# SBUF tiles on multiples of 128 bytes, small loads merged into one, and a fifth buffer for h, in a kernel of a spectral layer and two MLPs

## The chip, the core and the metric

The kernel runs on one NeuronCore of one Trainium2 chip. The metric is device time in microseconds (us) of one execution; lower is better. Times of several executions are given as a median with the lowest and the highest.

## The reference, cut to what matters

```python
def _attn_ref(x) -> np.ndarray:
    X = np.fft.fft(x, axis=1)
    X = np.fft.fft(X, axis=2)
    return X.real.astype(np.float32)
...
def _moe_ref(x, w_in, w_out) -> np.ndarray:
    h = x @ w_in
    r = np.maximum(h, 0.0)
    g = r * r
    return (g @ w_out).astype(np.float32)
...
def _moe2_ref(x, w_in, w_out) -> np.ndarray:
    h = x @ w_in
    g = h * (1.0 / (1.0 + np.exp(-1.702 * h)))
    return (g @ w_out).astype(np.float32)
```

The input x is 2 x 3008 x 256 in float32. The real part of its Fourier transform over positions and features gives 6016 tokens of 256 features. These go through an MLP with relu squared (weights 256 x 2048 and 2048 x 256) and then through one with a sigmoid gelu (the same sizes). Weights arrive as 64-bit floats and are narrowed on the chip.

## The kernel before, in words

Everything lies in SBUF as [128 partitions, columns]. Each partition holds a row of bytes, and pools take pieces of that row from the left end or from the right end.

The kernel has three stages, and they overlap. First, for each of the two batches, the positions are folded by VectorE (ops f0 to f5, lines 486 to 540), transformed by TensorE in plain float32 (lines 559, 571 and 643) and split into a high and a low float32r part, tile `eo` (pool `ep`). Then comes the first MLP: 96 units F0 to F95. A unit takes 128 hidden features of one block of tokens. A block is 2 x 512 tokens (64 units) or 2 x 482 tokens (32 units). A unit has 6 front matmuls (lines 770 to 772, moving operand `eo`) and 12 back matmuls (line 785, moving operands `gh` and `gl`, pool `mg`), each 512 or 482 columns wide in float32r. Between front and back, VectorE adds (op P, lines 1049 to 1052, into `h`), ScalarE or VectorE does relu and square (op R, lines 1058, or 1060 and 1061), ScalarE rounds to the high part (op H, line 1066), and GpSimd or VectorE makes the low part (op G, line 179). The back matmuls come three units later, so three units are left over at the end (`drain`). The second MLP has 48 units of 21 matmuls in line 1105 (moving operands `ya`, `yb`, `yc`) and 24 in line 1121 (moving operands `gh`, `gl` of pools `m2` and `m3`); 32 of these units are 512 columns wide and 16 are 482.

The order of all work up to the second MLP is written out by hand in `ORDER`: each engine's queue follows it, with the name of a unit or an op per item. `HOME` says which engine does an op where it isn't the usual one (V VectorE, A ScalarE, G GpSimd), and `RINGS` says which buffer of a group a tile takes. All DMAs are issued from SyncE's queue (SP) in the same order. The second MLP's order stands in its loop (lines 1131 to 1206).

Where tiles lie follows from the sizes. From the left: 1,024 bytes of DMA scratch, four constants of 32 bytes each, 1,344 bytes of pool `small`, then pools `winp` and `wq` (weights in float32r), all in pieces of 8,192 bytes; the first of these begins at byte 2,496, which is 64 above a multiple of 128. The right side ends at byte 229,344, which is 96 above a multiple of 128. Pools `mg`, `m`, `ep` and `np` are stacked downwards from there in pieces of 2,048, 4,096 or 8,192 bytes, so each of their tiles begins 96 above a multiple of 128. In the second MLP a 32-byte tile `edge` (line 1206) puts `m3` at 64 above a multiple of 128; `m2`, on the left, is at 64 too. The 376-column matmuls of line 747 read `eo` from column 106 on, that is 96 + 424 = 520 bytes, 8 above a multiple of 128.

Of the kernel before, what the change touches and what calls it, by code (L numbers as in the profile page):

```python
# [9 lines left out]
F32 = mybir.dt.float32  # L10
# [9 lines left out]
CW = 380  # L20
# [19 lines left out]
f0e0 f2a0 nA nL i0A f2m f2p nC seD f1E f1O f1e1 f2u i0L f0e1 c00D i0C i0O f2E f1e0 u0D nO f0o i0S f2e0 c01D i0P f1o e00N  # L40
i1D e00n ma f2O i0M f2o e00m f1g e00E u0L c02D u0A nS c03D i0N e00c u0O e01E u0C i0H u0S e01N e01c e00s f2e1 e01s e00h
u1D e00l i0l e01h e01n e01l i1L u0P nP f2g i1O u0H o0E0
F0 e01hb
F1 o0c0 c10D i1A u0l e01m u1A P0 P1 o0s0
F2 f0g R0 o0E1
F3 se e01lb H0 P2 i2D R1 o0c1 o0s1 o02hb o02h i1C G0 o02l P3 B0 o02lb H1 G1
F4 i1S R2 H2 o02N o02n G2 R3 u1C P4 H3 i1P R4 B1 f3D G3 H4
F5
F6 P5 B2 c12D u1L i1N B3 G4 P6 i1M u1O
F7 u1S R5 X3.0 X3.1 i1H u2D B4 R6 H5 i1l u1P P7 G5 H6 R7  # L50
F8
F9 P8 G6 R8 B5 P9 i2L
F10 H7 R9 i2A H8 P10 B6 G7 i2C
F11 u1H P11 H9
F12 R10
F13 u1l i2S i2O G8 G9 i2P P12 H10 P13 B7 B8 u2A R11 H11 u2L i2N B9
F14 i2M G10 B10 G11 R12 u2C i2H R13 i3D i2l H12
F15 P14 H13 i3A u2O B11 G12 G13
F16 X11.0 P15 R14 i3C u2S i3L
F17 X11.1 H14 G14 R15 B12 i3S u2P P16 u2H u3D B13  # L60
F18 u2l R16 i3O H15 B14 P17 P18
F19 H16 i3P
F20 G15 R17 P19 R18 H17 B15 H18 G16 i3M
# [60 lines left out]
F81 B74 P80 R78 B75 H77 v1S
F82 G77 v1L P81 H78 G78 v1O jlD R79 B76 H79 R80 R81 P82
F83 B77 G79 H80 H81 v1P R82
F84 G80 v1H B78 B79 G81 P83 P84 H82
F85 R83 X79.1
F86 G82 P85 X79.0 v1l R84 P86 B80 y0 H83 H84 G83 R85 B81 R86
F87  # L130
F88 B82 y1 P87 H85 G84
F89 R87 P88 G85
F90 P89 R88 B83 B84 H86 G86 ybH0
F91 B85 H87 H88 G87 P90 R89 P91 y2 ybl0
F92 G88 B86 H89
F93 G89 R90 P92 ybH1 P93 H90 yaH R91 B87
F94 B88 G90 ybl1 R92 H91 R93 G91
F95 yal y3 H92 P94 B89 P95 B90 H93 R94 R95 H94 G92 G93 B91 B92 H95 G94 G95
"""
RINGS = {  # L140
    "a0": "0101010101101010101010101010101010101010101011010101010101010101010101010101010100101010101010100010"
          "1010101010101010",
    "a1": "0110010101010101010101010101010101010101011010101101010101010101010101010101010101010101010101010101"
# [3 lines left out]
    "h": "0123021302130302130213023210321032031203120312031203120312031203120313120312031203120313120312031203"  # L147
          "1203311203120312",
    "p": "0111110101010101010101010101010101010101010101010101010101010101010101010101010101010101010101010101"
# [1196 lines left out]
```

## Time and profile before

| | |
|---|---|
| median of 3 runs | 954.26 us (954.04 to 956.01) |
| the profiled execution | 956.24 us |
| span of its trace | 954.4 us |
| TensorE matmul busy | 943.6 us, 99% of the span |
| TensorE weight load busy | 776.5 us, 81% |
| VectorE busy | 685.8 us, 72% |
| ScalarE busy | 572.8 us, 60% |
| GpSimd busy | 273.8 us, 29% |
| granted TensorE clock, mean over the span | 1.00 of full speed (2.4 GHz) |

The span is the time between the first and the last instruction of the program; 1.84 us of the profiled execution lie around it. PE is TensorE, PEld its weight load, DVE VectorE, ACT ScalarE, POOL GpSimd, SP SyncE's queue of DMAs. Matmuls are pipelined: the duration shown for one is longer than the distance between two starts, so the pace is read from starts, or from pieces of the chain that hold many matmuls.

### The profile page before, as it was taken

The page shows a single profiled execution, that of the slowest core. Times are in us where ns is not written, and L with a number is a line of the kernel's source. Part 1 is how long each engine was busy: PE and PEld are TensorE (multiplying, and loading weights), DVE is VectorE, ACT ScalarE, POOL GpSimd, SP SyncE. Part 2 cuts the span into 40 slices and gives each one's busy share as a digit, 9 for nine tenths or more (in the row PEclk, how much of TensorE's full clock was granted, in tenths as well). Part 3 has the DMA queues.
Part 4 walks back from the last instruction along what each step waited for, and adds up shares of the span by engine and source line. Part 5 has one row for each costly group of instructions (what it writes and reads, how often), then busy time and mean ns, then how long its engine had stood idle before and what let it go on. Part 6 is the DMA issues. An engine that isn't in the chain of part 4 may idle for free.

```text
span 954.4 us, 10920 instructions
## 1 busy us (share of the span) xinstructions
PE 943.6 (99%) x4272; PEld 776.5 (81%) x4272; DVE 685.8 (72%) x796; ACT 572.8 (60%) x613; POOL 273.8 (29%) x150
## 2 busy tenths in 40 slices
PE   8999999999999999999999999999999999999998
PEld 8668888887878878888788888888888888888886
DVE  7899998977767886758797755655565575566453
ACT  3779988566765868676765644644554455455343
POOL 0445665443266646474104200030020002000000
PEclk9999999999999999999999999999999999999999
DMA  7721222520110030110320110020010011000001
GB/s 285 270 89 45 88 89 89 202 88 25 45 42 1 1 133 1 45 45 1 109 110 1 42 45 1 3 86 1 0 65 22 1 42 45 0 1 37 8 1 41
DMA packets 13347, 53.47 MB, mean 56 GB/s; under 512 B 1520, under 2 KB 4976, under 8 KB 10096
## 3 DMA queue, kind: packets, MB, share of 16 engines
q1 hardware_dynamic: 13296, 52.78, 15.3%
q8 instruction: 33, 0.54, 0.2%
q14 instruction: 18, 0.15, 0.1%
HBM read 37.29 MB, written 15.48 MB: 55 GB/s over the span
## 4 chain that ended last, share of the span: by engine, by line
PE 93%; DVE 4%; DMA 1%; ACT 1%; issue 0%; POOL 0%; SPq 0%; DVEq 0%
PE psb L1121 27%; PE psb L785 26%; PE psc L1105 23%; PE psa L770 4%; PE psa L772 4%; PE psa L771 4%; PE psa L643 2%; PE psa L571 1%; DMA xt<-in_x 1%; PE psb L643 1%; DVE h L1052 0%; DVE h L1051 0%; DVE p L1049 0%; PE psb L571 0%; DVE h L1058 0%
## 5 line engine op out<-in xcount | busy, mean ns | idle before, releaser
L785 PE MATMUL psb<-gh,w 128*128 128x512 f32 (+1 forms) x768 | 219.0, 391 | 0.4 <-ACT o L275 0.4
L179 POOL TENSOR_TENSOR gl<-h,gh 128x1024 fp32r<-128x1024 f32 (+1 forms) x68 | 169.9, 2500 | 162.4 <-PE psb L785 72.8
L785 PEld LDWEIGHTS psb<-gh,w 128*128 128x128 f32 x768 | 143.4, 188 | 32.6 <-ACT o L275 1.2
L1121 PE MATMUL psb<-gh,w 128*128 128x512 f32 (+1 forms) x576 | 164.3, 387 | 0.0
L1185 DVE TENSOR_TENSOR g<-u,psc 128x1024 f32<-128x1024 f32 (+1 forms) x48 | 57.6, 1200 | 117.0 <-PE psc L1105 117.0
L1187 ACT ACTIVATE g<-g 128x1536 f32<-128x1536 f32 (+1 forms) x48 | 70.4, 1467 | 94.6 <-DVE g L1185 94.6
L1066 ACT CAST gh<-h 128x1024 fp32r<-128x1024 f32 (+1 forms) x96 | 97.9, 1030 | 47.3 <-PE psb L785 33.9
L1121 PEld LDWEIGHTS psb<-gh,w 128*128 128x128 f32 x576 | 108.3, 188 | 21.0
L785 PE MATMUL psb<-gl,w 128*128 128x512 f32 (+1 forms) x384 | 119.0, 391 | 0.0
L179 DVE TENSOR_TENSOR gl<-g,gh 128x2048 fp32r<-128x2048 f32 (+1 forms) x48 | 110.5, 2302 | 1.3 <-ACT gh L1162 1.3
L1051 DVE TENSOR_TENSOR h<-p,psa 128x512 f32<-128x512 f32 (+1 forms) x96 | 65.1, 678 | 44.7 <-POOL gl L179 29.8
L1060 ACT ACTIVATE h<-h 128x1024 f32<-128x1024 f32 (+1 forms) x79 | 82.3, 1041 | 22.2 <-DVE h L1052 22.2
L890 POOL TENSOR_TENSOR ue<-raw 128x512 f32<-128x512 f32 (+1 forms) x12 | 21.2, 1787 | 251.0 <-DMA raw<-ydram 244.6
L1162 ACT CAST gh<-g 128x2048 fp32r<-128x2048 f32 (+1 forms) x48 | 90.2, 1879 | 0.1
L1121 PE MATMUL psb<-gl,w 128*128 128x512 f32 (+1 forms) x288 | 88.1, 387 | 0.0
L785 PEld LDWEIGHTS psb<-gl,w 128*128 128x128 f32 x384 | 72.0, 188 | 15.9
L1061 ACT ACTIVATE h<-h 128x1024 f32<-128x1024 f32 (+1 forms) x79 | 82.7, 1047 | 2.5
L1049 DVE SCALAR_TENSOR_TENSOR p<-n,w1n_t,psa 128x512 f32<-128x512 f32 (+1 forms) x96 | 70.2, 732 | 10.4 <-PE psa L772 9.5
L770 PE MATMUL psa<-eo,w 128*128 128x512 f32 (+1 forms) x192 | 76.0, 396 | 1.1 <-DVE p L1049 0.6
L772 PE MATMUL psa<-eo,w 128*128 128x512 f32 (+1 forms) x192 | 75.1, 391 | 1.0 <-DVE w L179 1.0
L1184 ACT ACTIVATE g<-psc 128x512 f32<-128x512 f32 (+1 forms) x48 | 28.4, 591 | 78.5 <-PE psc L1105 78.5
L771 PE MATMUL psa<-eo,w 128*128 128x512 f32 (+1 forms) x192 | 75.0, 391 | 0.0
(164 smaller groups left out, 1499.6 us busy)
## 6 DMA issues: line engine op xcount, KB each, us to landing
ydram<-o SPq DMA_DIRECT2D x14, 512.0 KB, 2.8
xt<-in_x SPq DMA_DIRECT2D x5, 1024.0 KB, 8.3
cst<-in_dfts SPq DMA_DIRECT2D x8, 570.0 KB, 5.0
raw<-in_w1i SPq DMA_DIRECT2D x4, 1024.0 KB, 4.8
raw<-in_w1o SPq DMA_DIRECT2D x4, 1024.0 KB, 5.9
raw<-in_w2i SPq DMA_DIRECT2D x4, 1024.0 KB, 6.2
raw<-in_w2o SPq DMA_DIRECT2D x4, 1024.0 KB, 4.8
raw<-ydram SPq DMA_DIRECT2D x4, 1024.0 KB, 4.9
```

Of the source, the lines that this page charges most:

```text
L179: eng.tensor_tensor(out=o, in0=a, in1=f32(b), op=ALU.subtract)
L770: T.matmul(o, lhsT=w[:, 0, fs], rhs=t[:, par, 0, 0:wd], start=True, stop=False)
L771: T.matmul(o, lhsT=w[:, 0, fs], rhs=t[:, par, 1, 0:wd], start=False, stop=False)
L772: T.matmul(o, lhsT=w[:, 1, fs], rhs=t[:, par, 0, 0:wd], start=False, stop=True)
L785: T.matmul(acc[j][ec][:, s, 0:wd], lhsT=w[:, hl, e0:e0 + P], rhs=(gh, gl)[gi][:, s, 0:wd], start=(first and hl == 0 and gi == 0), stop=(la ...
L1060: A.activation(out=hv, in_=hv, func=AF.Relu)
L1061: A.activation(out=hv, in_=hv, func=AF.Square)
L1066: A.copy(st["gh"][:, :, 0:wd], st["h"][:, :, 0:wd])
L1105: T.matmul(bank, lhsT=w[:, hl, slot * P:(slot + 1) * P], rhs=x[:, yl, 0:wd], start=(first and hl == 0 and yl == 0), stop=(hl == 1), skip_g ...
L1121: T.matmul(o[:, s, 0:wd], lhsT=weights[1, 1, f // 4][:, hl, e0:e0 + P], rhs=g[:, 2 * i + s, 0:wd], start=(f == 0 and hl == 0 and g is gh), ...
L1162: A.copy(gh, gs[u - 1])
L1187: A.activation(out=g[:, 1:4], in_=g[:, 1:4], func=AF.Gelu_apprx_sigmoid)
```

## The change

The layout: row lengths of the transform's tables become multiples of 64 bytes (`CW`, `COLS`, tables `zc` and `zs`), the DMA scratch shrinks to 256 bytes, tiles `shift` (64 bytes, left) and `edge` (96 bytes, right) are put in, and small tiles move into a merged one. From the left, 256 + 128 + 1,024 bytes precede `winp`, which then begins at 1,408, a multiple of 128. From the right, 229,344 - 96 = 229,248 is a multiple of 128, and the sizes stacked below it are such that `mg`, `m`, `ep`, `np`, `cp`, `m2` and `m3` all begin on multiples of 128.

The loads: the feature table, the 128th features, the selector and the mask, which came by three DMAs (129, 24 and 64.5 KB), come by one of 232 KB into `misc`. The buffers: ring `h` has five tiles in place of four. The order: `ORDER` is written anew, as are the first DMAs, and ops change their engine in `HOME`. In `even_k`, the matmuls over all 128 rows of both parities come first and those over 64 rows after them. In the second MLP, `drain` is spread 2 and 1 over both of the first units, and the last copies to `gh` and `gl` are cut in two.

```diff
-CW = 380
+CW = 384
+SIN = 144
+COLS = [slice(0, 130), slice(SIN, SIN + P)]
...
-HOME = {**dict.fromkeys("""u0L j0L v0L v1L X3.1 X11.1 X47.1 X63.1""".split(), "A"), **dict.fromkeys("""f5s0 i0l u0l i3l u3l e01l e01lb o02l o02lb i2M i3M o03l e10l e11l o12l o12lb o13l y0 y1 y2 yal""".split(), "G"), **dict.fromkeys("""f3s0 f4s0 i1l u1l i0L o0c1 G1 R4 i2L R9 G9 G11 G12 i3L G16 G17 u3L G21 G26 G29 G32 R39 G38 G41 R45 R46 G44 G45 G48 R50 G49 G52 R55 o1c0 R59 R60 o12n G58 G59 R66 G65 R68 G69 R72 j13 G72 j1l1 G78 R81 R83 G88 R90 R91 G90 R94 G93 G94 G95""".split(), "V")}
+HOME = {**dict.fromkeys("""u0L v0L v1L X3.1 X11.1 X47.1 X63.1 X79.1""".split(), "A"), **dict.fromkeys("""f3s0 f5s0 i0l u0l i3l i1l u1l e01lb o02l o02lb i1M i2M i3M e11l o12lb o12l o13l y1 y2 y3 yal""".split(), "G"), **dict.fromkeys("""f4s0 u3l j0L o0c0 o0c1 o02n u1L G3 G6 u2L G9 R12 i2l G12 R16 G16 G19 G26 R32 G38 R42 R43 G41 e11n R45 R46 G44 R48 G45 G48 j02 j04 G51 R53 G53 o1c0 R56 G55 G56 R59 o12n G58 R63 G65 X63.0 R68 R69 G67 G68 G71 G72 R76 G74 R77 G75 G78 G79 G81 R82 G82 G86 R89 R91 G89 G92 R95 G93 G94 G95""".split(), "V")}
...
-f0D nyD f0Db dfD ny f1D df f0a0 nD f0s0 f0p f0a1 f0s1 f2D f0pb f0mb f0m f0E f1s0 f1a0 i0D f0Eb f1m f1p f1u f2s0 f0O f0Ob
...
+f0D f0Db f0s0 f0a0 dfD f0s1 f0p f0a1 f0m nD f1D f0pb f0mb df nL f0E f0Eb f2D ny f1a0 f0O f1s0 f0Ob f0e0 f1p i0D f1m f1u
...
-    "h": "0123021302130302130213023210321032031203120312031203120312031203120313120312031203120313120312031203"
...
+    "h": "0123402134021302413024130132401324032140321401432013240132401324013243201432014320143202114302143021"
...
+    small.tile([P, 16], F32, name="shift")
...
+    edge = tc.alloc_tile_pool(name="edge", bufs=1, side="right")
+    edge.tile([P, 24], F32, name="edge")
...
+    misc = zp.tile([P, 464], F32, name="misc")
+    x128_t = misc[:, 272:320].rearrange("p (q a) -> p q a", q=6)
+    mask = misc[:, 448:449]
...
-    x128_t = small.tile([P, 6, 8], F32, name="x128_t")
...
-    mask = small.tile([P, 1], F32, name="mask")
...
-        ne = small.tile([P, 6, 4], F32, name="ne")
-        nu = small.tile([P, 6, 2], F32, name="nu")
+        w = m.tile([P, NP], F32, **of("p", 2), name="na")
+        ne, nu = (w[:, lo:lo + 6 * n].rearrange("p (q a) -> p q a", q=6) for lo, n in ((0, 4), (24, 2)))
...
-        consts["dft"] = zp.tile([P, 2, 258], F32, tag="dft", name="dft")
-        nc.sync.dma_start(consts["dft"][:, 0], dftd)
-
-    @op("df")
-    def _():
-        A.mul(consts["dft"][:, 1], consts["dft"][:, 0], -1.0)
-
-    @op("nyD")
-    def _():
-        nc.sync.dma_start(x128_t, x128)
+        nc.sync.dma_start(misc, miscd)
 
     @op("nD")
     def _():
         nc.sync.dma_start(w1n_raw, w1n.bitcast(U32))
 
-    @op("seD")
+    @op("df")
     def _():
-        consts["sel"] = m.tile([P, NP], F32, **of("p", 2), name="sel_raw")
-        nc.sync.dma_start(consts["sel"][:, 0:P + 1], sel)
-
-    @op("ma")
-    def _():
-        A.copy(mask, consts["sel"][:, P:P + 1])
+        consts["minus"] = zp.tile([P, 272], F32, name="minus")
+        A.mul(consts["minus"], misc[:, 0:272], -1.0)
+
+    def features(minus, par):
+        return (consts["minus"] if minus else misc)[:, COLS[par]]
 
     @op("se")
     def _():
-        A.copy(sel_t, consts["sel"][:, 0:P])
+        A.copy(sel_t, misc[:, 320:448])
...
-                t[b] = zp.tile([P, NC, 4, n], F32, tag=("zc", "zs")[n == P], name=("zc", "zs")[n == P])
+                w = zp.tile([P, 1568 if n > P else 1536], F32, tag=("zc", "zs")[n == P], name=("zc", "zs")[n == P])
+                t[b] = w[:, 0:NC * 4 * n].rearrange("p (c s l) -> p c s l", c=NC, s=4)
...
-            for par, (z, slot) in enumerate(((zc[b], kb), (zs[b], 1 - kb))):
-                halves(*(pe[:, h, 256 * par:256 * par + hw] for h in range(2)),
-                       [(z[:, :, slot, 0:P], cs[:, :, 190 * par:190 * par + hw])], par == 0)
+            for full in (True, False):
+                for par, (z, slot) in enumerate(((zc[b], kb), (zs[b], 1 - kb))):
+                    for h, (c, p0, p1) in enumerate((EVEN[not full], ODD[full])):
+                        T.matmul(pe[:, h, 256 * par:256 * par + hw], lhsT=z[p0:p1, c, slot, 0:P],
+                                 rhs=cs[p0:p1, c, 192 * par:192 * par + hw], start=(full and par == 0), stop=not full,
+                                 skip_group_check=True)
...
+    def halves_of(u):
+        return (slice(0, 2), slice(2, 4)) if u >= units - 1 else (slice(0, 4),)
...
-                A.copy(gh, gs[u - 1])
+                for at in halves_of(u):
+                    A.copy(gh[:, at], gs[u - 1][:, at])
...
-                for d in drain[0:3 - 2 * u]:
+                for d in drain[0:2]:
...
-                for d in drain[3 - 2 * u:3]:
+                for d in drain[2:3]:
...
-                sub(V, gl, gs[u - 1], gh)
+                for at in halves_of(u):
+                    sub(V, gl[:, at], gs[u - 1][:, at], gh[:, at])
...
-        m3.tile([P, 8], F32, tag="edge", name="edge")
...
-        out[kb, :, 190:190 + n] = np.where(((t >= 1) & (t <= 375 + kb))[:, None], np.sin(angle), 0.0)
+        out[kb, :, 192:192 + n] = np.where(((t >= 1) & (t <= 375 + kb))[:, None], np.sin(angle), 0.0)
...
+    misc = np.zeros((P, 464), np.float32)
+    misc[:, 0:272] = _dft_features()
+    misc[:, 272:320] = x128.reshape(P, 48)
+    misc[0, 320:448] = 1.0
+    misc[1:, 448] = 1.0
...
-    nc = bacc.Bacc("TRN2", target_bir_lowering=False, num_devices=1, dynamic_dma_scratch_size=1024)
+    nc = bacc.Bacc("TRN2", target_bir_lowering=False, num_devices=1, dynamic_dma_scratch_size=256)
```

## Rows read from the trace of the kernel before

**Rows 1.** Stretches: busy us (count) of PE, PEld, DVE, ACT, POOL; clock, DMA share, GB/s.

```profile
0.00:16.00 16.00, 13.37 (x99) 13.02 (x100) 9.76 (x21) 2.84 (x8) 0.20 (x4) 1.00 0.87 330
...
36.00:50.00 14.00, 14.00 (x59) 9.92 (x58) 12.65 (x23) 12.24 (x17) 7.73 (x7) 1.00 0.52 193
50.00:60.00 10.00, 10.00 (x46) 8.16 (x45) 9.76 (x11) 6.24 (x8) 5.66 (x3) 1.00 0.01 2
60.00:70.00 10.00, 8.35 (x34) 5.84 (x33) 9.66 (x12) 9.10 (x10) 2.56 (x2) 1.00 0.51 179
70.00:150.00 80.00, 79.48 (x341) 63.64 (x341) 75.99 (x97) 69.14 (x70) 50.34 (x21) 1.00 0.22 77
```

**Rows 2.** The chain that ended last, whole span: start, length, what.

```profile
83.40 8.40 PE psb L785 x36
...
198.78 7.92 PE psb L785 x36
...
486.99 2.72 PE psb L1121 x12
```

**Rows 3.** The same chain, from 924 to 932 us.

```profile
926.33 2.64 PE psb L1121 x12
```

**Rows 4.** TensorE's timeline around two pairs of 376-column matmuls: start, length, what.

```profile
147.63 0.51 PE L747 MATMUL psa<-eo,sel_t 128*128 128x376 f32 x2
147.99 0.62 PE L785 MATMUL psb<-gh,w 128*128 128x512 f32 x2
...
361.74 0.51 PE L747 MATMUL psa<-eo,sel_t 128*128 128x376 f32 x2
362.08 0.39 PE L770 MATMUL psa<-eo,w 128*128 128x512 f32 x1
```

**Rows 5.** What TensorE waited for: us in total, times, longest.

```profile
PE psa L571 <- DVE xt L521: 1.4, 1, 1.4
...
PE psa L772 <- DVE w L179: 1.0, 1, 1.0
PE psa L770 <- DVE p L1049: 0.6, 1, 0.6
PE psc L1105 <- DVE g L1154: 0.5, 1, 0.5
...
PE psb L1121 <- DVE gl L179: 0.3, 1, 0.3
```

**Rows 6.** TensorE's timeline where the second MLP begins.

```profile
468.37 0.87 PE L1105 MATMUL psc<-yc,w2i 128*128 128x512 f32 x3
469.77 1.43 PE L1105 MATMUL psc<-yc,w2i 128*128 128x512 f32 x5 [0.54 <-DVE g L1154]
```

**Rows 7.** TensorE's timeline, an even block of the second batch.

```profile
227.80 1.32 PE L643 MATMUL psa<-cst,zc 128*128 128x188 f32 x8
229.05 1.42 PE L643 MATMUL psa<-cst,zs 128*128 128x188 f32 x8
230.40 0.49 PE L770 MATMUL psa<-eo,w 128*128 128x482 f32 x1
```

**Rows 8.** SyncE's first DMA issues.

```profile
1.24 0.45 SPq L453 DMA_DIRECT2D x_t<-in_x  x1
...
2.21 0.47 SPq L445 DMA_DIRECT2D dft<-in_dftd  x1
2.72 0.43 SPq L236 DMA_DIRECT2D xt<-in_x  x1
```

**Rows 9.** VectorE's timeline, the first and last op on the 128th features, and the second fold.

```profile
4.92 0.18 DVE L425 TENSOR_TENSOR ne<-x_t 128x24 f32<-128x24 f32 x1 [3.92 <-DMA x_t<-in_x]
...
5.71 0.18 DVE L431 TENSOR_SCALAR nyq<-nyq 128x24 f32<-128x24 f32 x1
...
11.12 1.23 DVE L490 TENSOR_TENSOR t<-xt 128x1024 f32<-128x1024 f32 x1 [0.91 <-DMA xt<-in_x]
```

**Rows 10.** VectorE's low parts of 1,024 columns in the first MLP: count, busy us, mean ns.

```profile
L179 DVE TENSOR_TENSOR gl<-h,gh 128x1024 fp32r<-128x1024 f32 x18 | 22.3, 1243 | 0.3 <-PE psb L785 0.3
```

More of the change, by code (lines that the diff above doesn't have):

```diff
@@ new lines @@
+e01N e01s e00h nS e00l e01h e01hb u0H f1g i1C e01n nP u0l u1A i1O o0E0 e01l e01m
+F0
+F1 P0 i1S e01lb R0 o0E1 o0c0
+F2 P1 o0s0 H0
+F3 R1 o0c1 o0s1 G0 o02h P2 o02hb o02l B0 o02lb P3 H1 o02N R2
+F4 R3 o02n i2D H2 u1C i1P G1
+F5 P4 i1M P5 H3 G2 u1L R4 u1S i1N R5 B1 H4 G3
+F6 i1H u1O G4 B2 B3 X3.0
+F7 X3.1 H5 i1l B4 P6 u1P
+F8 u2D P7 G5 P8 R6 u1H H6
+F9 P9 i2L u1l G6 i2A R7 i2C H7 i2O
+F10 B5 R8 R9 P10 u2L B6 H8 G7 i2S i2P G8
+F11 P11
+F12 R10 H9 P12 R11 B7 i2N
+F13 G9 H10 R12 i2M P13 H11 u2A G10 B8
@@ new lines @@
+F14 u2C G11 B9 P14 i2H R13
+F15 H12 R14 u2S i3D u2O B10 i2l G12 H13 P15 G13 B11 X11.0 X11.1
+F16 B12 H14 o03h
+F17 u2P R15 i3A P16 u2H R16 B13 o03l H15 i3L H16 G14
+F18 u2l B14 P17 P18
+F19 i3C i3O R17 G15 B15 i3S R18
+F20 H17 u3D G16 B16 i3P H18 u3A f3D P19 u3L P20
+F21 i3M P21 c11D G17 u3C R19 B17 G18 H19 o03N
+F22 i3N R20 o03n H20 i3H R21 G19 G20 P22 Y19
+F23 u3O P23 i3l B18 B19 u3S H21
+F24 G21
+F25 X19.0 X19.1 P24 B20 R22 H22 G22 u3P R23 P25
+F26 P26 B21 H23 R24 R25 f3a0 u3H H24 f3s0 f3m R26 G23
@@ new lines @@
+F27 f3p P27 B22 G24 H25
+F28 R27 P28 u3l B23
+F29
+F30 H26 B24 f3v P29 H27 G25 G26 B25 v0D
+F31 P30 G27 B26 R28 f4D f3u H28 P31 R29 f3w B27 G28 H29 G29 Y27 X27.0 R30 H30 f3O R31 X27.1
+F32 H31 f3o G30 B28 f3E f4s0 P32 G31
+F33 f4a0 f4m f4p c10D B29 R32 H32 B30 f4v f3e1 P33
+F34 f4u f4w f5D B31 G32 P34 Y31 f3e0 R33 H33 G33 X31.0 X31.1 R34 f4E
+F35 f4e1 P35 H34 R35 B32 f4e0
+F36 c12D
+F37 H35 P36 P37 f5a0
+F38 G34 R36 f5s0 B33
+F39 H36 P38 f5m R37 B34 G35 P39 f5p
+F40 R38 f5u P40 f4O G36 f5v f4o H37 B35 H38 G37 R39 f5w
@@ new lines @@
+F41 B36 P41 f5E f3g
+F42 f5e0 f5O R40 H39 H40 f5e1 P42 B37 e10N f5o R41
+F43 e10n e10m G38 R42 G39 e10E =x B38 f4g H41 P43 e10c G40 R43
+F44 B39 e10s H42 G41 P44
+F45 e11E e10h G42 R44 e10l j0D P45 e11N e11c e11n B40 H43 e11s e11m R45 e11h
+F46 H44 e11l
+F47 P46 B41 R46 G43 P47
+F48 B42 e11hb R47 P48 e11lb
+F49 H45
+F50 H46 G44 j0A B43 R48 B44 G45 G46 P49 j0C
+F51 P50 j0S B45 P51 H47 B46 G47 H48 j0L G48 R49
+F52 B47 R50 H49
+F53 j0O H50 G49 j0P R51 j01 X47.0 X47.1 P52 G50 B48 j02
+F54 P53 j03 H51 B49 P54 j04
@@ new lines @@
+F55 B50 R52 G51 H52
+F56 f5g j0H0 j0H1 c13D B51 G52 P55 R53 P56 H53 R54
+F57 R55 j0l0
+F58 P57 j0l1 G53 B52 o1E0 P58 o1c0 o1E1 o1s0
+F59 H54 G54 R56 H55 G55 o1c1 R57 o1s1 P59
+F60 o12hb B53 H56 P60 G56 o12lb B54 o12h o12l
+F61 o12N P61 H57 B55 R58 R59 H58
+F62 R60 G57 H59 o13h o12n
+F63 R61 o13l B56 H60 G58 P62
+F64 v0L P63 R62 R63 B57 G59 G60
+F65 v0A P64 B58 H61 H62
+F66 v0O P65 R64 G61 B59
+F67 H63 v0C G62 P66 =c R65 R66
+F68 P67 B60 H64 G63 v0S B61 H65 B62 G64 B63 v0P R67 H66 P68
+F69 G65 X63.0
@@ new lines @@
+F70 P69 P70 v0H G66 j1D
+F71 X63.1 R68 R69 B64 v1D v0l B65
+F72 H67 P71
+F73 R70 j1A G67 H68 G68 P72 B66 H69 H70 P73 R71 B67 j1L G69 R72
+F74 G70
+F75 P74 R73 B68 j1O j1C j1S B69 P75 j1P
+F76 H71 B70 j11 G71
+F77 H72 j12 H73 j13 P76 R74 B71 G72 j14 P77 B72 o13N R75 j1H0 R76 G73 H74 H75 o13n H76 G74 j1H1
+F78 j1l0 B73 R77 yD j1l1 B74 v1A v1L
+F79 G75 H77 G76 G77 P78 P79
+F80 P80 R78 B75 v1C H78 v1O
+F81 P81 B76 B77 G78
+F82
+F83 R79 H79 R80 G79 P82 B78 H80 R81 P83
+F84 B79 P84 H81 G80 v1S
+F85 G81 X79.0 R82 X79.1 B80 H82 R83
@@ L558, in part_half @@
                     if at == half:
-                        T.matmul(o, lhsT=v[:, par, j], rhs=consts["dft"][:, minus, cols],
+                        T.matmul(o, lhsT=v[:, par, j], rhs=features(minus, par),
                                  start=(not half and i == 0 and s in ((0, 2) if par == 0 else (0,))),
@@ L570, in part @@
                 for i, (v, j, minus) in enumerate(of_s):
[L571 removed]
+                    T.matmul(o, lhsT=v[:, par, j], rhs=features(minus, par),
                              start=(i == 0 and (s % 2 == 0 if par == 0 else s == 0)), stop=(i == len(of_s) - 1),
@@ L642, in halves @@
                         lhsT = lhsT.to_broadcast([p1 - p0, P])
-                    T.matmul(o, lhsT=lhsT, rhs=const[p0:p1, c], start=(fresh and full and i == 0),
+                    T.matmul(o, lhsT=lhsT, rhs=const[p0:p1, c], start=(full and i == 0),
                              stop=(not full and i == len(terms) - 1), skip_group_check=True)
```

137 lines of the change are left out of this document (22 added, 115 removed).

## The prediction

> **What bounds the kernel now.** I read the engines' busy times by stretch first, then the chain that ended last, then TensorE's waits. TensorE is the bound: from 70 us on it is busy without a break except for a few waits of under a microsecond, at a granted clock of 1.00, the 2.4 GHz level [rows 1, 5]. From 36 to 70 us VectorE is nearly as full (32.07 of 34 us), and so it is from 70 to 150 us (75.99 of 80) [rows 1]. So the time is a number of matmuls times their pace, plus a start. The reader is to look at the pace, and not at busy time, since busy time counts the pipeline twice.
>
> **The pace.** In the first MLP 36 back matmuls of 512 columns take 8.40 us, 233.3 ns or 560 cycles each, and 36 of 482 columns take 7.92 us, 220.0 ns or 528 cycles [rows 2]. In the second MLP 12 of 512 columns take 2.72 us, 226.7 ns or 544 cycles, and 12 of 482 columns 2.64 us, again 528 cycles [rows 2, 3]. The same shape runs at two paces, and the shorter one does not. What differs is where the moving operand begins: 96 bytes above a multiple of 128 in the first MLP, 64 above in the second. Count the 64-byte lines that it touches. 512 columns are 2,048 bytes: 32 lines from 64 above, 33 from 96 above (32 + 2,048 is 32.5 lines). 482 columns are 1,928 bytes: 31 lines from either start. Then all four paces are 16 x (lines + 2) cycles: 35, 34, 33 and 33 times 16. That is a fit on four points, and I take it as the forecast's rule.
>
> **The change, part by part.**
>
> *Tiles on multiples of 128.* In the first MLP 64 units x 18 = 1,152 matmuls of 512 columns go from 33 to 32 lines: 16 cycles or 6.67 ns each, 7.68 us. The 576 of 482 columns keep their 31 lines, and so do all 2,160 of the second MLP their lines: nothing. About 100 of the 1,152 run between 36 and 70 us (139 records, less some 40 of the transform and the selection), where VectorE sets the pace as much [rows 1]; I leave out 0.7 us for these and take 7.0. If 70 to 150 us gave nothing either (341 records x 6.67 ns = 2.3 us) it would be 4.7. VectorE had 4.0 us free there, so I keep that part.
>
> *What the last 64 bytes do.* No row shows a 512-column matmul from a multiple of 128. The bounds are nothing (the rule above, for which 64 and 128 are alike) and, on the other side, a rule that fits the four points as well: if the read begins at the 128-byte line and only one extra step is paid, a start at 64 or 96 carries one step of 16 cycles that a start at 0 does not. The nearest row is the selection, whose operand lies 8 above a multiple of 128. Two of 376 columns (24 lines) need 0.36 us in one place and 0.34 in the other [rows 4], 0.175 each on the mean. The first rule gives 26 x 16 cycles, 173 ns, the second 25 x 16, 167 ns. The row is nearer to the first, though its two places are 0.02 apart, so I take nothing here and keep the other end for a rival.
>
> *The drain, 2 and 1 in both units.* In the second unit of the second MLP three matmuls begin at 468.37 and the next at 469.77, where 3 x 0.227 = 0.68 us would have done: 0.72 us lost, because only 6 back matmuls cover VectorE's three additions [rows 6]. Now 12 do, 1.32 us more. I take 0.7, with 0 and 0.7 as bounds; what is late next would be the following unit's first matmuls, which keep 6 back matmuls of cover.
>
> *The last copies in halves.* The last wait for `gl` is 0.3 us, and the weight load behind it adds some [rows 5]. I take 0.4, bounds 0 and 0.5.
>
> *Even blocks, full rows first.* Two halves of a block take 1.25 and 1.35 us from start to start; the second follows a 64-row pair, and that switch costs 0.10 [rows 7]. One switch each way goes, in four blocks: 0.4 us, bounds 0 and 0.8.
>
> *The fifth `h`, and engines.* The low parts that move between VectorE and GpSimd cost 1.24 us each [rows 10], and before unit F24 seven of them stood on VectorE and six stand there now; relu-squares on VectorE are two before and two after. With the weights' and the transform's ops counted at the durations of like ops, VectorE has about 1.5 us less in all, an estimate. The new buffer can save no more than the waits in the first 70 us after the start, 0.6 for `p` and part of 1.0 for a weight's low part [rows 5]. I take 0.5, bounds 0.5 lost and 2 gained.
>
> *Merged loads.* SP loses two issues of about 0.45 us [rows 8], but the second fold's load stays the fifth issue, so it starts no earlier, and 95 KB more go ahead of it (512 + 512 + 232 + 16 against 24 + 512 + 512 + 129 KB): 0.29 us at 330 GB/s [rows 1]. VectorE stood idle 0.91 us before that fold, and TensorE waited 1.4 us behind it [rows 5, 9]. The six small ops on the 128th features (4.92 to 5.89 us) move into that idle time. Cost 0.3, bounds 0 and 0.8, the upper one if those ops also push the fold.
>
> The sum: -7.0 - 0.7 - 0.4 - 0.4 - 0.5 + 0.3 = -8.7 us. Against the profiled execution, 956.24 us, that is 947.5. It stands 1.98 us above the median, so against the median, 954.26, it is 945.6 us. With the bounds the forecast's own range is 941 to 950.
>
> **The rivals.**
>
> *The last 64 bytes count (0.30).* Then a matmul of 512 columns takes 528 cycles and one of 482 takes 512. First MLP: 1,152 x 13.33 ns + 576 x 6.67 = 19.2 us; second: 1,440 x 6.67 + 720 x 6.67 = 14.4; together 33.6. Between 36 and 150 us VectorE has only 5.9 us free [rows 1], and 480 records at 13.33 ns are 6.4 us, so I leave out 3.0. With the other parts (-1.7) that is -32.3: 922.0 us, between 918 and 927. For it: the fit is as good, and one of the two selections. Against it: their mean, and a rule that rounds the front to 128 bytes but the end to 64.
>
> *Where a tile lies does nothing (0.08).* The paces would differ between the MLPs for another reason, and -1.7 is left: 952.6 us. Against it: 482 columns run equally in both, which a difference between the stages would not do.
> The Trainium skill speaks for this rival: SBUF — State Buffer, section Specifications (TRN2), gives lines of 16 bytes. All starts here (96, 64 and 0 above 128) are multiples of 16, so by that page alone 512 columns are 128 lines from each of them, and the layout would be worth nothing. The trace disagrees so far, with 560 against 544 cycles.
> The skill's page TensorE: Matmul & The Clock Gate, section Back-to-back issue gap, gives N / 2.4 + 2.5 ns, that is 215.8 ns for 512 columns; no row here is that fast (226.7 is the least).
>
> *VectorE becomes the bound early (0.07), slower than before.* From 36 to 150 us TensorE had 2.2 us idle and VectorE 5.9 [rows 1]. The new order could make each of some 24 units in that stretch wait for VectorE, as two units did, 0.5 to 1.0 us at a time [rows 5]. At 0.5 us each that is 12 us: 945.6 + 12 = 957.6. It decides from 8.7 us lost, 0.36 a unit. For it: VectorE at 95% from 70 to 150 us, with GpSimd's ops behind it. Against it: VectorE is given slightly less, and in that stretch TensorE was kept waiting 0.5 us in all.
>
> **How the numbers follow.** The forecast has 0.55 at 945.6 us. A change of 0.2% (1.9 us) is about what a measurement of this kernel can tell from none. Faster: 0.55 + 0.30 + half of 0.08 + 0.02 of the slow case, 0.91. Same: the other half, 0.04, and 0.01. Slower: 0.04. The range runs from 918, which takes in nearly all of the first rival, to 951 above the forecast's own; the likeliest case has 941 to 950.
>
> **What would show it.** Right: 36 back matmuls of 512 columns in the first MLP in 8.16 us, 482 columns still 7.92, and the second MLP's pieces still 2.72 and 2.64; no wait near the second MLP's second unit; the second fold 0.3 us later. If the last 64 bytes count, the pieces of 12 read 2.64 and 2.56 in both MLPs. If 8.40 stays, where a tile lies does nothing. If VectorE is the bound, TensorE's busy time drops below the stretch's length between 36 and 150 us, with waits for `p` and `h`. The prediction is wrong if the pace has a part that the four points can't show, or if the new order's waits outweigh 8.7 us.

## The result, and the profile after

The changed kernel takes 944.38 us (median of 4 runs, 944.23 to 944.70) against 954.15 us of the kernel before (median of 4, 953.06 to 956.01). The ratio is 0.990, with a 95% interval of 0.9888 to 0.9913. That is 9.8 us faster; 8.7 was forecast, and 944.38 lies inside the forecast's own range. The rule behind the largest term is wrong all the same, as the experiments show.

The profiled execution of after is 944.28 us with a span of 942.5. TensorE's matmuls are busy for 934.3 us of it (99%), VectorE for 697.9. The chain that ended last, whole span of after (start, length, what):

```profile
55.00 5.44 PE psb L783 x24
...
240.24 5.28 PE psb L783 x24
...
462.14 2.73 PE psc L1103 x12
```

The same chain of after, where the last unit ends:

```profile
920.03 2.64 PE psb L1119 x12
...
924.65 13.21 PE psb L1119 x60
```

Line 785 is now 783, line 1105 is 1103, line 1121 is 1119. In the first MLP 24 back matmuls of 512 columns take 5.44 us, 226.7 ns or 544 cycles each, where they took 560 [rows 2]. The 482 columns (5.28 for 24) are at 220.0 ns as before, and the second MLP's pieces of 12 are unchanged too, at 2.73 and 2.64 us [rows 2, 3]. Only the one pace has moved.

Stretches of after, columns as in [rows 1]:

```profile
36.00:50.00 14.00, 14.00 (x62) 10.26 (x62) 13.22 (x23) 11.11 (x13) 6.57 (x5) 1.00 0.06 25
50.00:60.00 10.00, 10.00 (x46) 8.29 (x45) 9.63 (x14) 9.01 (x10) 5.68 (x3) 1.00 0.01 2
60.00:70.00 10.00, 10.00 (x45) 8.28 (x45) 8.45 (x13) 9.54 (x11) 9.17 (x4) 1.00 0.59 210
70.00:150.00 80.00, 79.74 (x352) 65.76 (x351) 77.05 (x94) 70.88 (x72) 51.80 (x20) 1.00 0.29 102
```

TensorE's idle time from 36 to 150 us has gone from 2.17 us [rows 1] to 0.26, though it runs faster in that stretch. What TensorE still waited for in after (us in total, times, longest):

```profile
PE psa L444 <- DVE still L267: 1.1, 1, 1.1
PE psa L638 <- DVE h L1050: 0.8, 1, 0.8
PE psa L769 <- DVE eo L181: 0.6, 1, 0.6
PE psb L638 <- ACT eo L650: 0.5, 1, 0.5
PE psa L768 <- DVE zc L594: 0.3, 1, 0.3
PE psa L768 <- DVE h L1050: 0.3, 1, 0.3
```

The waits for the second fold (1.4), for a weight's low part (1.0), for `p` (0.6), for `g` in the second MLP (0.5) and for the last `gl` (0.3) are gone [rows 5]. Waits for `h`, `eo` and `zc`, 0.3 to 0.8, stand there now.

VectorE's timeline of after, the first and last op on the 128th features, and the second fold:

```profile
8.92 0.18 DVE L431 TENSOR_TENSOR na<-misc 128x24 f32<-128x24 f32 x1
...
9.70 0.18 DVE L437 TENSOR_SCALAR nyq<-nyq 128x24 f32<-128x24 f32 x1
9.82 1.23 DVE L490 TENSOR_TENSOR t<-xt 128x1024 f32<-128x1024 f32 x1
```

The second fold begins at 9.82 us, not at 11.12 [rows 9], and without a wait.

TensorE's timeline of after, one even block and the start of the next:

```profile
23.55 0.91 PE L673 MATMUL psa<-cst,zc 128*128 128x189 f32 x4
24.29 0.80 PE L673 MATMUL psa<-cst,zs 128*128 128x189 f32 x4
25.02 0.59 PE L673 MATMUL psa<-cst,zc 64*128 64x189 f32 x4
25.45 0.49 PE L673 MATMUL psa<-cst,zs 64*128 64x189 f32 x4
25.86 0.90 PE L673 MATMUL psb<-cst,zc 128*128 128x188 f32 x4
```

From 23.55 to 25.86 it is 2.31 us. The 16 records of a block took 2.60 before (227.80 to 230.40, in the second batch) [rows 7].

### The profile page after: what moved, and what is told of

The parts are those of the page before. It is cut to its first block, busy times and chain, and to the rows that moved or that the text cites. A ratio compares the mean times of both kernels' runs of the same rounds, so it can differ in the third digit from the quotient of the medians.

```text
span 942.5 us, 10895 instructions
## 1 busy us (share of the span) xinstructions
PE 934.3 (99%) x4272; PEld 778.5 (83%) x4272; DVE 697.9 (74%) x810; ACT 566.8 (60%) x605; POOL 267.8 (28%) x144
## 4 chain that ended last, share of the span: by engine, by line
PE 97%; DVE 2%; DMA 1%; ACT 0%; issue 0%; SPq 0%; DVEq 0%
PE psb L1119 27%; PE psb L783 27%; PE psc L1103 24%; PE psa L768 5%; PE psa L769 5%; PE psa L770 5%; PE psa L638 1%; PE psa L565 1%; PE psa L673 1%; PE psb L638 1%; DMA xt<-in_x 1%; PE psb L565 0%; DVE eo L181 0%; DVE h L1050 0%; DVE t L486 0%; DVE t L490 0%
## 5 line engine op out<-in xcount | busy, mean ns | idle before, releaser
L783 PE MATMUL psb<-gh,w 128*128 128x512 f32 (+1 forms) x768 | 216.0, 387 | 0.0
L181 POOL TENSOR_TENSOR gl<-h,gh 128x1024 fp32r<-128x1024 f32 (+1 forms) x62 | 155.7, 2514 | 136.9 <-PE psb L783 74.6
L181 DVE TENSOR_TENSOR gl<-g,gh 128x2048 fp32r<-128x2048 f32 (+2 forms) x50 | 110.7, 2217 | 0.4 <-ACT gh L1164 0.4
L1058 ACT ACTIVATE h<-h 128x1024 f32<-128x1024 f32 (+1 forms) x76 | 79.2, 1042 | 23.8 <-DVE h L1050 23.8
L1164 ACT CAST gh<-g 128x2048 fp32r<-128x2048 f32 (+2 forms) x50 | 90.5, 1814 | 0.1
L1059 ACT ACTIVATE h<-h 128x1024 f32<-128x1024 f32 (+1 forms) x76 | 79.7, 1049 | 2.4
```

The costliest lines, as they stand in the source:

```text
L181: eng.tensor_tensor(out=o, in0=a, in1=f32(b), op=ALU.subtract)
L783: T.matmul(acc[j][ec][:, s, 0:wd], lhsT=w[:, hl, e0:e0 + P], rhs=(gh, gl)[gi][:, s, 0:wd], start=(first and hl == 0 and gi == 0), stop=(la ...
L1058: A.activation(out=hv, in_=hv, func=AF.Relu)
L1059: A.activation(out=hv, in_=hv, func=AF.Square)
L1164: A.copy(gh[:, at], gs[u - 1][:, at])
```

## The experiments

In what follows the place of a tile is given by its byte address modulo 256. All weight tiles of the MLPs begin at one such residue (the left side), the moving operands `eo`, `gh` and `gl` at another (the right side); in the second MLP `ya` and `yb` (in the weights' own pools), `yc` and every second `gh` (in `m2`) lie on the left. "Distance" is the difference of the two residues. From the sizes in the text on the kernel before: weights at 192, moving operands of the first MLP at 224 (distance 32), of the second at 192 (distance 0). After: 128 on both sides, distance 0 in both MLPs. So the rule of the prediction (lines touched by the moving operand) and a rule by the distance give the same four paces, and only new layouts tell them apart.

Ratios are to runs of the kernel before on the same chip. The median of before was 956.28 to 957.02 us in those sets, 954.15 beside after, so a kernel as fast as after has a ratio near 0.987 there. After itself was not run again in those sets; where a time is set against its 944.38, two sets are compared.

### Both sides on multiples of 64

After, with the last 64 bytes taken back on each side: weights at 64, moving operands at 192, distance 128.

```diff
-    small.tile([P, 16], F32, name="shift")
-    edge.tile([P, 24], F32, name="edge")
+    edge.tile([P, 8], F32, name="edge")
```

> The changed kernel with all tiles 64 bytes back, on 64 above a multiple of 128 at both sides. Line rule (16 x (64-byte lines + 2) cycles): every matmul keeps its lines, 226.7 ns for 512 columns and 220.0 for 482 in both MLPs, so the changed kernel's 944.4 us within 0.5. Rival, the last 64 bytes count somewhere (TensorE's operands, or the DMAs into the tiles): slower than 944.4 by 1 us or more; if the earlier second fold of the changed kernel comes from the 128-byte starts, the fold falls back by up to 1.2 us.

Measured: 954.33 us (953.94 to 954.63, 11 runs), ratio 0.9985 (0.9976 to 0.9995). The chain, whole span:

```profile
55.13 5.57 PE psb L782 x24
```

24 matmuls of 512 columns take 5.57 us, 232.1 ns or 557 cycles each (other pieces of this chain 560). By the line rule a start at a multiple of 64 has 32 lines and 544 cycles, so the line rule is refuted. The last 64 bytes, for which the prediction took nothing, are worth 9.95 us from here (954.33 - 944.38), though no pace fell under 544.

### The first MLP's moving operands 32 bytes off

After, with only the first MLP at distance 32 again (weights 128, moving operands 160):

```diff
-    edge.tile([P, 24], F32, name="edge")
+    edge.tile([P, 16], F32, name="edge")
...
+        m3.tile([P, 8], F32, tag="edge", name="edge")
```

> The changed kernel with the right side at 32 above a multiple of 64 in the first two stages; the second MLP's right-side tiles are put back on multiples of 128. Line rule: 1,152 matmuls of 512 columns in the first MLP touch a 33rd line, 233.3 ns in place of 226.7, 7.0 to 7.7 us more: 951.4 to 952.1 us; 482 columns stay at 220.0. Rival, the layout does nothing and order and loads made the gain: 944.4 us.

Measured: 950.83 us (950.75 to 951.16, 5 runs), ratio 0.9943 (0.9929 to 0.9956). The chain, whole span:

```profile
55.35 5.60 PE psb L783 x24
```

The 512 columns are back at 560 cycles. So the layout is worth 6.45 us in the new order; the prediction had 7.0.

### The kernel before with one tile of 32 bytes

The kernel before, its order and loads untouched, with 32 bytes put in on the right: moving operands at 192, distance 0, on a multiple of 64 and not of 128.

```diff
+    edge = tc.alloc_tile_pool(name="edge", bufs=1, side="right")
+    edge.tile([P, 8], F32, name="edge")
...
-        m3.tile([P, 8], F32, tag="edge", name="edge")
```

> The kernel before with a 32-byte tile at the right end, which puts the first MLP's operands on 64 above a multiple of 128 and changes nothing else. Line rule: 12 matmuls of 512 columns in the first MLP take 2.72 us in place of 2.80; 7.0 us less, 947.1 us, less if VectorE sets the pace up to 150 us (4.7 us less, 949.5). Rival, the layout does nothing: 954.2 us.

Measured: 946.75 us (945.75 to 949.80, 5 runs), ratio 0.9905 (0.9889 to 0.9921). The chain, whole span:

```profile
79.83 8.16 PE psb L787 x36
```

8.40 us for 36 [rows 2] has become 8.16, 544 cycles each. Most of the change's gain comes from one tile of 32 bytes.

### Paces by themselves, first try

> All of the kernel's work is left out; 24 float32r matmuls in a row for each of 512, 482, 480 and 376 columns, with the moving operand 0, 8, 16, 32, 48, 60, 64 and 96 bytes above a multiple of 128, then with shifted weights, one weight tile, bfloat16 and float32. Line rule, 16 x (lines + 2) cycles: 512 columns 226.7 ns from 0 and 64, 233.3 from all other starts; 482 columns (1,928 bytes) 220.0 from 0 to 48, 64 and 96, and 220.0 from 60 too with 31.06 lines rounded up to 32: 226.7; 480 columns 213.3 from 0 and 64, 220.0 from the others; 376 columns 173.3 from 0 to 32, 64 and 96, 180.0 from 48 and 60. Weights' place: no change. Rival, the front is rounded to 128 bytes and one step is paid: 512 columns 220.0 from 0, 226.7 from 64, 233.3 from 96; 376 columns 166.7 from 8. Rival, 17 cycles a line: 376 columns 170 ns, 480 columns 212.5. Rival, lines of 16 bytes: 8 and 60 above slower than 16, 32 and 48.

With the 480-column matmuls at some 517 to 535 cycles, where 30 lines would give 512, the line rule falls here too. Lines of 16 bytes fare no better: of the eight starts of 512 columns the one at 60 bytes, no multiple of 16, was the fastest, with 544 cycles against 551 to 563. But in this kernel the two weight tiles lay at different residues, so it does not settle what the distance does. It suggests that the effect belongs to float32r: plain float32 (256 columns) took 518 cycles a pass from starts at 0 and 32 bytes alike, and bfloat16 is in its timeline:

```profile
200.25 10.31 PE L43 MATMUL o<-half,wh 128*128 128x512 bf16 x47
210.40 0.38 PE L43 MATMUL o<-raw 128*128 128x256 f32 x1
```

47 matmuls in 10.15 us are 216.0 ns each, from a start at 0 and from one at 32 bytes alike. Both used a single weight tile, the float32r runs two in turn, and no other start was tried.

### The left side moved, the right side left alone

After, with the weights 32 bytes back, at 96: distance 32. What else lies on the left, `ya`, `yb`, `yc` and every second `gh` of the second MLP, moves with them. Every moving operand on the right, all those of the first MLP among them, stays on a multiple of 128.

```diff
-    small.tile([P, 16], F32, name="shift")
+    small.tile([P, 8], F32, name="shift")
```

> The changed kernel with the left side 32 bytes back: weights, and the second MLP's left-side operands, begin 352 above a multiple of 512, the right side 384. Line rule (the moving operand's 64-byte lines alone): first MLP unchanged at 226.7 ns for 512 columns; line 1103 and the left-side part of line 1119 at 233.3; some 6 us more, 950.6. New theory, the distance between weight and moving operand modulo 256 bytes sets the pace, zero being the good one: first MLP 233.3 ns (7.7 us more); line 1103 has both operands on the left and stays at 226.7; line 1119 with operands on the right 233.3, on the left 226.7 (3.4 us more): about 955.5.

Measured: 955.83 us (955.68 to 956.35, 10 runs), ratio 0.9996 (0.9985 to 1.0007): 11.45 us slower than after. The chain, whole span:

```profile
55.39 5.60 PE psb L783 x24
```

The first MLP is at 560 cycles with its moving operands where they were. A rule that looks at the moving operand alone can't give that.

### Both sides 32 bytes off

The same weights at 96, and the right side moved with them: distance 0, nothing on a multiple of 64 or 128.

```diff
-    small.tile([P, 16], F32, name="shift")
+    small.tile([P, 8], F32, name="shift")
...
-    edge.tile([P, 24], F32, name="edge")
+    edge.tile([P, 32], F32, name="edge")
```

> The changed kernel with both sides on 32 above a multiple of 64 (352 above a multiple of 512). Line rule: all 2,592 matmuls of 512 columns touch 33 lines, 233.3 ns, 17 us more: 961.7. Distance theory: the distance is 0 as in the changed kernel, 226.7 everywhere: 944.4 within 0.5.

Measured: 944.27 us (944.21 to 945.14, 4 runs), ratio 0.9874 (0.9851 to 0.9896). The chain, whole span:

```profile
55.87 5.44 PE psb L783 x24
```

It equals after within 0.2 us. The multiples of 128 themselves are worth nothing.

### Both sides on 64, level

As in the first experiment both sides lie on multiples of 64, but at the same residue, 64.

```diff
-    small.tile([P, 16], F32, name="shift")
...
-    edge.tile([P, 24], F32, name="edge")
+    edge.tile([P, 40], F32, name="edge")
```

> The changed kernel with both sides on 64 above a multiple of 128, as in the first experiment, but with the right side another 128 bytes further in, so that both sides are 320 above a multiple of 512. Distance theory: 226.7 ns everywhere and 944.4 us within 0.5, against 954.3 of the first experiment. Rival, tiles at 64 above a multiple of 128 are slow by themselves once five h tiles and the new order are there: 954.3.

Measured: 944.26 us (944.14 to 944.52, 4 runs), ratio 0.9872 (0.9846 to 0.9899). The chain, whole span:

```profile
54.85 5.44 PE psb L782 x24
```

Beside the 954.33 of the first experiment this is the cleanest pair: the same alignment, distance 128 or 0, 10.1 us apart.

### Paces by distance

> All of the kernel's work is left out; 24 float32r matmuls in a row of 512 and of 482 columns, weights at a multiple of 512 bytes, the moving operand 0 to 240 bytes above one in steps of 16, then with both shifted by 32, 64 and 128 bytes, and with the moving operand further on by whole multiples of 256. Distance theory: 226.7 ns at distance 0, also when both are shifted and at distances 256 and 512; other distances reach up to 233.3, 32, 96 and 128 among them; 482 columns 220.0 at 0, 32 and 96. Line rule: 226.7 from 0, 64, 128 and 192, 233.3 from all others, and 220.0 for 482 columns.

Cycles from start to start (24 matmuls, weights alternating between two tiles at one residue), worked out from the first and the last of 24 starts in the timeline:

| distance | 0 | 16 | 32 | 64 | 96 | 128 | 160 | 192 | 224 | 240 |
|---|---|---|---|---|---|---|---|---|---|---|
| 512 columns | 544 | 556 | 560 | 550 | 561 | 559 | 561 | 559 | 559 | 545 |
| 482 columns | 529 | 523 | 528 | 528 | 528 | 528 | 522 | 522 | 528 | 514 |

With both operands shifted together by 32, 64 or 128 the 512 columns stay at 547 to 548; at 256 and 512 they are at 544 again. At distance 240 the 512 columns are as fast as at 0, and the 482 columns are at their fastest, which no theory had forecast. Its 24 of 512 columns and its 24 of 482, each with the first matmul of the next group, in the timeline:

```profile
99.74 0.40 PE L40 MATMUL o<-halfhundredtwelve,wa 128*128 128x512 f32 x1
...
105.18 0.38 PE L40 MATMUL o<-zero,wa 128*128 128x482 f32 x1
...
184.11 0.39 PE L40 MATMUL o<-halfhundredtwelve,wa 128*128 128x482 f32 x1
...
189.26 0.40 PE L40 MATMUL o<-thirtytwo,wa 128*128 128x512 f32 x1
```

5.44 / 24 is 226.7 ns, 544 cycles; 5.15 / 24 is 214.6 ns, 515 cycles with the switch to the next group in it.

### The small loads apart again

After, with `misc` loaded by three DMAs at their old places in SP's queue; layout and order of the rest untouched.

```diff
-f0D f0Db f0s0 f0a0 dfD ... f1p i0D f1m f1u
+f0D nyD f0Db f0s0 f0a0 dfD ... f1p i0D seD f1m f1u
...
-        nc.sync.dma_start(misc, miscd)
+        nc.sync.dma_start(misc[:, 0:272], miscd[:, 0:272])
...
+        nc.sync.dma_start(misc[:, 272:320], miscd[:, 272:320])
...
+        nc.sync.dma_start(misc[:, 320:464], miscd[:, 320:464])
```

> The changed kernel with the merged load cut again into three DMAs at the places of before (128th features second, feature table fourth, selector and mask after the second weights). If the merged load is what lets the second fold begin at 9.9 us in place of 11.1, the fold falls back by 1.2 us and the time is 945.6 us. If the order of the ops did it, 944.4 us within 0.3.

Measured: 945.56 us (945.26 to 945.91, 4 runs), ratio 0.9882 (0.9868 to 0.9897), 1.2 us slower than after. VectorE's timeline:

```profile
7.38 0.69 DVE L494 TENSOR_TENSOR t<-xt 128x512 f32<-128x512 f32 x1 [1.17 <-DMA xt<-in_x]
...
10.80 1.22 DVE L498 TENSOR_TENSOR t<-xt 128x1024 f32<-128x1024 f32 x1
```

VectorE waits 1.17 us for the second half of the first input, and the second fold begins at 10.80 instead of 9.82. The 24 KB of small rows stand between the two halves of the first input again, and packets under 512 bytes in the first 16 us number 412 in place of 255. Which of the two does it, the place in the queue or the packets, these runs don't separate. The second fold itself waits for no load here, only for VectorE's own earlier ops.

### Everything at distance 240

The kernel before with 32 bytes on the right, the even blocks, the drain and the halves of after, and all float32r moving operands but `ya` and `yb` read from 240 bytes into larger tiles:

```diff
+    def ahead(tl, n):
+        return tl[:, 60:60 + n * NP].rearrange("p (a k) -> p a k", a=n)
...
-            st["gh"] = mg.tile([P, 2, NP], F32R, **of("gh", 4), name="gh")
+            st["gh"] = ahead(mg.tile([P, 1088], F32R, **of("gh", 4), name="gh"), 2)
...
-    yC[0] = m2.tile([P, 2, 3, NP2], F32R, tag="yc", name="yc")
+    yC[0] = ahead(m2.tile([P, 3136], F32R, tag="yc", name="yc"), 6).rearrange("p (h i) k -> p h i k", h=2)
```

> The kernel before, its order and loads kept, with the right side on the weights' remainder modulo 256 and all moving tiles but those of ya and yb read from 240 bytes further on; even blocks, drain and last copies as in the changed kernel. Distance theory with the paces measured alone: 512 columns 226.7 ns as at distance 0, 482 columns 213.3 in place of 220.0 in the first MLP (576, 3.8 us), in line 1121 (384, 2.6 us) and for yc (144, 1.0 us); 946.75 of the third experiment less 7.4, less about 2 for the three edits: 937.3. If the pace measured alone does not hold in the kernel, where pairs of matmuls share a weight: 944.7 or more.

Measured: 953.29 us (951.13 to 953.60, 6 runs), ratio 0.9956 (0.9944 to 0.9969): a miss of 16 us. The chain, whole span:

```profile
80.73 8.52 PE psb L793 x36
...
170.34 8.16 PE psb L793 x36
...
246.39 7.68 PE psb L793 x36
```

The 482 columns met the forecast, 7.68 / 36 = 213.3 ns or 512 cycles. The 512 columns did so only in part. At one and the same distance they run at three paces, each for many units: 236.7 ns or 568 cycles from 70 to 146 us (8.52 / 36), 233.3 ns (2.80 for 12) after the two selections at 145.9 us, and 226.7 ns or 544 cycles from 170 us on (8.16 / 36), once the fronts are 482 columns wide; later 568 and 560 come back. The measurement by itself had 544.

### One row back

> All of the kernel's work is left out; 24 float32r matmuls in a row of 512, 482 and 496 columns, weights at a multiple of 512 bytes, the moving operand 0 to 64 bytes short of a multiple of 256, and then with each weight used by two matmuls in a row. Distance theory: at 16 short, 512 columns 226.7 ns and 482 columns 213.3, as measured at 240; with weights in pairs the same. Nothing is forecast for the steps in between.

The same distance of 240, in another succession of runs. 24 matmuls of 512 columns, and the first of the next group:

```profile
38.88 0.40 PE L41 MATMUL o<-sixteen,wa 128*128 128x512 f32 x1
...
44.55 0.40 PE L41 MATMUL o<-twenty,wa 128*128 128x512 f32 x1
```

5.67 / 24 is 236.3 ns, 567 cycles, and 482 columns took 528; with each weight used twice in a row it was 560 and 529. Both forecasts missed. So the residue does not fix the pace at 240. Distance 0 gave 544 here too (546 with weights in pairs), but it is not the only fast place: 4 and 20 bytes short of it, 512 columns took 544 and 545.

### The distance by the width

As "everything at distance 240", but the 512-column operands back at distance 0:

```diff
-    def ahead(tl, n):
-        return tl[:, 60:60 + n * NP].rearrange("p (a k) -> p a k", a=n)
+    def ahead(tl, n, wd):
+        at = 0 if wd == NP else 60
+        return tl[:, at:at + n * NP].rearrange("p (a k) -> p a k", a=n)
```

> The kernel of the last experiment but one (order of before, distance 240), with the moving operands of 512 columns back at distance 0 and only those of 482 columns at 240. Its own paces are expected to meet: 512 columns 226.9 ns as at distance 0, 482 columns 214.2 as measured at 240. Against 953.3 us there, 1,152 x 6.5 ns in the first MLP and 768 x 5.8 and 288 x 6.4 in the second, 13.8 us less: 939.5 us, below the changed kernel's 944.4. If a pace hangs on the matmuls before it rather than on the distance, 482 columns go back to 220.0 and the time is 946 us.

Measured: 940.43 us (939.93 to 943.57, 5 runs), ratio 0.9836 (0.9823 to 0.9849), faster than after. The chain, whole span, and its end:

```profile
81.90 8.16 PE psb L794 x36
...
194.30 7.68 PE psb L794 x36
...
244.70 7.92 PE psb L794 x36
...
924.22 12.81 PE psb L1131 x60
```

The time is near the first forecast, 939.5, though both cases came true in part. Most of the second MLP's 482 columns keep 213.5 ns (12.81 / 60). In the first MLP they begin at 213.3 (7.68 / 36 at 194.30 us) and fall back to 220.0 (7.92 / 36 at 244.70 us). In between, from 233.75 us on, fronts of 512 columns come in, at distance 0 now and at 240 in the run before, where 213.3 went on. In the second batch the back matmuls of 482 columns are at 220.0 too (399 to 446 us), although the fronts among them are 482 columns wide and at 240 again. So the fronts beside them do not set the pace alone; a pace, once taken, mostly goes on. This kernel has the order of the kernel before and its waits (in the profiled execution, 943.57 us, TensorE is idle 2.58 us between 60 and 70 us). The same layout with the new order and the merged load was not run.

## Why the prediction was right, and where it was wrong

**The bound** was read rightly: TensorE sets the time, and the pace of the 512-column matmuls in the first MLP was the thing to look at. Nothing else in the chain changed its pace.

**The pace's rule** fails: "what differs is where the moving operand begins". What differs is where it begins against the weights. The layouts that tell the two apart all go with the distance: 64 against 192 is slow, 96 against 96 and 64 against 64 are as fast as 128 against 128, and the left side moved alone is slow. The prediction had four points and a rule with one free reading; the weights' address stood in the text on the kernel and was not used.

**Tiles on multiples of 128** were sized well, since the step from 560 to 544 was taken from rows and not from the rule: 7.0 forecast, 6.45 measured in the new order and 7.4 in the old (946.75 against 954.15). The reason is that the change levels the two sides, not that they are on 128. That the number held is luck: for both sides on 64 and a distance of 128 the same rule forecasts the same time, and it missed by 9.95 us.

**The last 64 bytes** were taken at nothing "for which 64 and 128 are alike". The rival that they bring 528 and 512 cycles is refuted by the second MLP, still at 544 and 528. But they are not worth nothing either: `shift` moves the left side up and `edge` moves the right side down, so 64 bytes each turn a distance of 128 into 0, and 9.95 us hang on them.

**The drain, and the last copies.** At the second unit of the second MLP the nine matmuls that held the gap of [rows 6] now run through, and the last 60 back matmuls take 13.21 us, 220.2 ns each, with no wait. TensorE's timeline of after:

```profile
458.17 0.60 PE L783 MATMUL psb<-gh,w 128*128 128x482 f32 x2
458.61 2.21 PE L1103 MATMUL psc<-yc,w2i 128*128 128x512 f32 x9
460.66 0.59 PE L783 MATMUL psb<-gh,w 128*128 128x482 f32 x2
```

From 458.61 to 460.66 it is 2.05 us for nine, 227.8 ns each. The two edits together can be read off, since the second MLP's paces are the same in the kernel before and in after. The chains, whole span, of its first piece and its last: before,

```profile
455.48 2.76 PE psc L1105 x12
...
939.56 10.39 PE psb L1121 x46
```

the kernel before with one tile of 32 bytes,

```profile
445.73 2.74 PE psc L1107 x12
...
929.81 10.40 PE psb L1123 x46
```

and after,

```profile
444.68 2.73 PE psc L1103 x12
...
924.65 13.21 PE psb L1119 x60
```

From the first start to the end of the last it is 494.47, 494.48 and 493.18 us: 1.3 us less where the two edits are in, with 0.7 and 0.4 forecast. Neither was undone alone.

**Even blocks** were mis-sized. 0.29 us of TensorE's time are saved in the block shown, so four blocks give about 1.2 us and not 0.4, outside the bound of 0.8. The prediction took the 0.10 of the way back to 128 rows for the price of all switches that go. How much of it reaches the kernel's time is open, since it was not undone alone.

**Merged loads** have the wrong sign: +0.3 forecast, -1.2 measured. The step that failed is "it starts no earlier, and 95 KB more go ahead of it". The load is issued no earlier, at 2.72 us in both kernels [rows 8], and 95 KB more go ahead of it, yet it was there by 9.82 us and not only at 11.12. So the bytes ahead did not set when it landed. In the kernel with the loads apart the first fold's second half comes 1.17 us late, and all behind it, the second fold included, follows.

**The fifth `h` and the engines** were given 0.5. From the kernel before with one tile of 32 bytes, which has the old order, to after it is 2.37 us between medians. Of these the drain and the halves are 1.3 and the merged load is 1.2, so nothing is left for the even blocks, the fifth `h` and the engines together, within a scatter of some 2 us. The medians hide what they did bring. In the old order a kernel's times spread over 2.5 to 5.2 us within a set, in the new one over 0.4 to 0.9. TensorE's busy time between 60 and 70 us in the third experiment and in the last one, both in the old order:

```profile
60.00:70.00 10.00, 9.49 (x42) 7.46 (x41) 9.27 (x13) 8.94 (x9) 4.29 (x3) 1.00 0.60 210
60.00:70.00 10.00, 7.42 (x29) 4.75 (x27) 9.66 (x13) 7.96 (x9) 2.56 (x2) 1.00 0.54 210
```

It stood idle there for 0.51 and 2.58 us, for 1.65 in the kernel before [rows 1] and for 0.34 with everything at distance 240. In after and the six full kernels made from it, it did not stand idle there at all. So the new order took out a wait whose length changed from run to run. Whether the order, the engines or the fifth `h` did it is open.

The number came out 1.2 us from the measured one because errors met: the loads (1.5 us) and the even blocks (0.8, if they count in full) on one side, a layout 0.55 smaller and nothing for the fifth `h` on the other. How near it really is hangs on the kernel before: its four runs beside after have a median of 954.15 us, the 47 runs of the other sets medians of 956.28 to 957.02, while the two levelled layouts there repeat after's time within 0.2 us. Against those sets the gain is 12 us, where 8.7 was forecast.

**The rivals.** That a tile's place does nothing is refuted by the 32-byte tile alone. VectorE did not become the bound: it was busy 77.05 of 80 us from 70 to 150 us, more than before, and TensorE lost 0.26 us.

**What stays open.** Why distance 0 is fast, and why distance 240 gives 544 and 512 cycles in some successions and 560 to 568 and 528 in others. What ran before goes along with it, as both kernels at distance 240 show, but no run isolates it. A new order with four buffers for `h` was not tried.

## What to carry to other kernels

For float32r matmuls of 512 columns, put the moving operand and the weights at the same address modulo 256 bytes before looking at anything finer; it cost one tile of 32 bytes here, and alignment to 64 or 128 alone bought nothing. (The full kernels that show it are level modulo 512 too; a difference of 256 was tried in one group of 24 matmuls.) When a rule is fitted to the paces of a profile, list every address that the instruction reads, not only the one that the change moves, and try a layout on which the candidates disagree. For loads at the start, look at what stands between the halves of the first input rather than at the bytes ahead. And look at the spread between runs as well as at the median: here it goes along with a wait of 0.3 to 2.6 us that no single trace shows to vary.

## What the runs showed of the hardware

A float32r matmul's pace depends on where its two operands lie against each other. For 512 columns it is 544 cycles at distance 0 and 550 to 562 at every other multiple of 16 bytes up to 224; for 482 columns 522 to 530. In the kernel, the left side moved by 32 bytes alone took the first MLP's 512 columns from 544 to 560 cycles, with their moving operands where they were, and cost 11.45 us of 944 in all.
The Trainium skill, SBUF — State Buffer, section Who interferes with whom, gives TensorE two read ports, one for the moving operand and one for weights, and calls them independent. For float32r these runs differ from that in so far as the pace hangs on both addresses together; where the two reads meet, no run shows.

bfloat16 did not show it from the two starts tried, 0 and 32 bytes: 216.0 ns for 512 columns from either.
The Trainium skill, TensorE: Matmul & The Clock Gate, section Back-to-back issue gap, gives 215.8 ns for an isolated one, and the trace agrees for bfloat16. No group of float32r matmuls of 512 columns came under 226.7 ns.

And the pace of a float32r matmul at distance 240 is not fixed by the distance: in one kernel 512 columns ran at 236.7, 233.3 and 226.7 ns, and in another 482 columns of the first MLP ran at 213.3 ns until fronts of 512 columns came in, and at 220.0 ns from then on. Each of these paces went on over several units.
